# RWKV-6 attention followed by a squared-ReLU feed-forward: attention products in two groups per step, block-diagonal pair state, two shared PSUM banks, whole-group casts

## The chip, the cores and the metric

One core of one Trainium2 chip. The metric is the device time of one execution in microseconds (us); the time of a kernel is the median of its runs. Engines are called as in the profile: PE (TensorE; PEld its weight loads), DVE (VectorE), ACT (ScalarE), POOL (GpSimd), SP (SyncE, which here issues the DMAs).

## The reference, cut to what matters

```python
# r, k, v, w: (4 batches, 8 heads, 768 positions, 48); u: (8, 48)
for t in range(S):
    cur = einsum('bhd,bhe->bhde', u * k[t], v[t])
    y[t] = einsum('bhd,bhde->bhe', r[t], state + cur)
    state = w[t][..., None] * state + einsum('bhd,bhe->bhde', k[t], v[t])
x = y.transpose(0, 2, 1, 3).reshape(3072, 384)
out = relu(x @ w_in) ** 2 @ w_out        # w_in (384, 2048), w_out (2048, 384)
```

Inputs and output are float32; the products run in bfloat16 with float32 sums.

## The kernel before, in words

The 4 x 768 positions are cut into 12 steps of 256 (`T`), three per batch (`NB = 3`); a step is two chunks (`c`) of 64 partitions with two neighbouring positions (`j`) on each partition. The heads go in four pairs (`HP`, index `p`, head of the pair `e`), each head padded from 48 to 64 rows (`DP`).

**Attention of one step s.** `ww_`, `rw_`, `kw_` multiply decays into w, r and k; `lw_` takes the logarithm; `cum_` (L213) sums the logarithms on PE; `exp_` (L222) makes decay factors, and the chunk's total decay `a_c`; `rd_` (L229) writes the decayed r and k into `rdec`. `tr_`/`rkt_` transpose them through PSUM for steps 0 to 3, `dtr_` (L256) by a DMA transpose from step 4 on. `p_` (L261) forms k-times-r products for two head pairs at once in 64x64 tiles, `pm_` (L273) masks them. `su_` (L281) sums k-times-v over a chunk, one 64x64 product per head; `ts_` (L295) adds the old state, `sn_` (L303) multiplies by `a_c` on POOL and gives the next state `S`, two heads one above the other, 48 columns each. `y_` (L329) adds the inner products (mask times v, 32 products in 64x128 tiles) and, through `carried` (L320), the old state's share of the even heads (64x64 tiles); `yb_` adds the odd heads' share and the bonus term u (`ku_`, `qp_`, `q_`, `vq_`, then four `spread` products of 384 columns). For steps 0 and 1 a small DVE copy `yw_` stands between `y_` and `yb_`. `ysb_` evicts y; `yt_`/`xt_` (steps 0 to 3) or `dyt_` (L371, DMA transpose) turn it into x.

**Feed-forward (MoE) of one step.** `m1_` (L380): eight groups of 12 products with w_in; `rl_` relu, `sq_` square; `m2_` (L405): for each half of 128 rows four groups of four products with w_out; `os_` (L413) scales and evicts, `store` (L417) issues two DMAs on SP.

**PSUM.** `att` is two double banks; cum, p, su and y each take one and give it back after `rd_`, `pm_`, `ts_`, `ysb_`. One bank serves all transposes, two serve `m1_`, one serves `m2_` (and the warm-up products of L424, which fill PE's waits ahead of the first m2).

**Order.** All engines run in an order that is written when the kernel is built: `plan` (L431 to L550) lists every piece of work with engine, planned duration, rank, inputs and PSUM needs; `make_order` (L559) plays it through with these durations, on each engine taking the ready piece of lowest rank. Attention of step s has ranks around 200 s, its MoE 700 later. The order is then fixed: each engine works through its list, and a piece that waits holds up all behind it. Loads go through SP in the order `seq` (L525): steps 0 and 1 (w r u k v, w r k v), four w_in blocks, step 2, four w_out blocks, then steps 3 to 11. A load waits for the buffers of four steps earlier, and w of step n also for `y_(n - 3)`. On SP the ranks put transposes first, then stores, then loads. Weights come as float32 blocks of 768 KB and are cast a column group at a time: 12 casts for w_in, 16 for w_out, on ACT or DVE (L113).

Of the kernel before, what the change touches and what calls it, by code (L numbers as in the profile page):

```python
# [18 lines left out]
def kernel(  # L19
# [17 lines left out]
    C = 128  # L37
# [75 lines left out]
    def cast(kind, g, j):  # L113
        dst = wi_sb[:, :, g * GW:(g + 1) * GW] if kind == "i" else wo_sb[:, g * 4:(g + 1) * 4, :]
        copy = nc.scalar.copy if where["cast", kind, g, j] == "A" else nc.vector.tensor_copy
        copy(dst[:, j], w_st[kind, g][:, j])
# [34 lines left out]
    for i in range(NLW):  # L151
        t = consts.tile([C, H, DP], BF16, name=f"lw_buf{i}")
        nc.gpsimd.memset(t[:], 0.0)
        lw_bufs.append(t)
    NRD = 2
# [27 lines left out]
    def v_(s):  # L183
        v_bf = tiles["v", s] = a_mid.tile([C, H, 2, D], BF16, name="v_bf", bufs=3)
        nc.scalar.copy(v_bf[:], raw["v", s][:])  # L185
# [36 lines left out]
    def exp_(s):  # L222
        cs = tiles["cs", s]
        a_c = tiles["a_c", s] = a_small.tile([C, HP, 2], FP32, name="a_c")
        nc.scalar.activation(
            a_c[:], cs[:, 0, DM:DM + 2 * HP].rearrange("p (a c) -> p a c", c=2), AF.Exp)
        nc.scalar.activation(cs[:, :, 0:DM], cs[:, :, 0:DM], AF.Exp)  # L227

    def rd_(s, i):  # L229
        if i == 0:  # L230
            tiles["rdec", s] = rdec_bufs[s % NRD]
        rdec, cs = tiles["rdec", s], tiles["cs", s]
        x = raw["rk"[i], s][:, :, 0:3:2, :]
        nc.vector.tensor_mul(  # L234
            rdec[:, i, :, :, 0:D], x.rearrange("p h j d -> p j h d"),
            cs[:, i, 0:DM].rearrange("p (h d) -> p h d", h=H)[:, None, :, :].to_broadcast([C, 2, H, D]))
        if i == 1:
            del tiles["cs", s]

    def tr_(s, i):  # L240
        rdec = tiles["rdec", s]
        ps_tr = tiles["tr", s] = ps_tr_pool.tile([C, 2, HP, C], BF16, name="tr")
# [4 lines left out]
    def new_rkt(s, i):  # L247
        if i == 0:
# [3 lines left out]
    def rkt_(s, i):  # L252
        copy = nc.scalar.copy if where["rkt_", s, i] == "A" else nc.vector.tensor_copy
        copy(new_rkt(s, i)[:, i], tiles.pop(("tr", s))[:])
# [18 lines left out]
    def pm_(s, f):  # L273
        if f == 0:
# [5 lines left out]

    def su_(s):  # L281
        rdec, v_bf = tiles["rdec", s], tiles["v", s]
        ps_su = tiles["su", s] = att[slot["su_", s]]
        n_c = 1 if s % NB == NB - 1 else 2
        for j in range(2):
            for p in range(HP):
                for c in range(n_c):
                    for e in range(2):
                        part = slice(c * Q, (c + 1) * Q)
                        nc.tensor.matmul(ps_su[e * DP:(e + 1) * DP, c, p * D:(p + 1) * D],  # L290
                                         rdec[part, 1, j, 2 * p + e, :], v_bf[part, 2 * p + e, j, :],
                                         start=(j == 0 and p == 0), stop=(j == 1),
                                         skip_group_check=True)

    def ts_(s, c):  # L295
        ps_su = tiles["su", s][:, c, 0:HP * D].rearrange("p (a d) -> p a d", a=HP)
        ts = tiles["ts", s, c] = a_mid.tile([C, HP, D], FP32, name="t_state")
        if s % NB == 0 and c == 0:
            nc.vector.tensor_copy(ts[:], ps_su)
        else:  # L300
            nc.vector.tensor_add(ts[:], tiles["S", s, c][:], ps_su)  # L301

    def sn_(s, c):  # L303
        t = tiles["S", s + c, 1 - c] = a_mid.tile([C, HP, D], BF16, name="S", bufs=6)
        nc.gpsimd.tensor_mul(t[:], tiles.pop(("ts", s, c))[:],  # L305
                             tiles["a_c", s][:, :, c:c + 1].to_broadcast([C, HP, D]))


# [10 lines left out]

    def carried(s, e):  # L320
        rows = slice(e * DP, (e + 1) * DP)
        for p in range(HP):
            h = 2 * p + e
            for c in range(0 if s % NB else 1, 2):
                for j in range(2):
                    y_mm(s, c, slice(h * D, (h + 1) * D), tiles["rkT", s][rows, 0, j, p, c * Q:(c + 1) * Q],
                         tiles["S", s, c][rows, p, :], j)

    def y_(s):  # L329
# [10 lines left out]
        carried(s, 0)  # L340

    def yw_(s):
        seen = a_small.tile([1, 2], FP32, name="seen")
        nc.vector.tensor_copy(seen[:], tiles["y", s][0:1, :, 0])

    def yb_(s):
        vq = tiles.pop(("vq", s))
        carried(s, 1)
# [10 lines left out]
    def yt_(s):  # L359
        y_sb = tiles.pop(("ysb", s))  # L360
        ps_yt = tiles["yt", s] = ps_tr_pool.tile([C, 2, KT, C], BF16, name="tr")
# [4 lines left out]
    def xt_(s):  # L366
        xT = tiles["xT", s] = xt_pool.tile([C, 2, KT, C], BF16, name="xT")
        copy = nc.scalar.copy if where["xt_", s] == "A" else nc.vector.tensor_copy
        copy(xT[:], tiles.pop(("yt", s))[:])
# [35 lines left out]
    def m2_(s, c, q):  # L405
        gt = tiles["gt", s]
        if q == 0:
            tiles["m2"] = ps_m2.tile([C, DM], FP32, name="m2")
        for n in range(4 * q, 4 * q + 4):
            nc.tensor.matmul(tiles["m2"][:], gt[:, n, c * C:(c + 1) * C], wo_sb[:, n, :],  # L410
                             start=(n == 0), stop=(n == NT - 1))

    def os_(s, c):  # L413
        o_sb = tiles["o", s, c] = o_pool.tile([C, DM], FP32, name="o_sb")
        nc.scalar.activation(o_sb[:], tiles.pop("m2")[:], AF.Copy, scale=1.0 / (RS * RS))  # L415

    def store(s, c):  # L417
# [3 lines left out]
        for j in range(2):  # L421
            nc.sync.dma_start(out=rows[j], in_=o_sb[j * Q:(j + 1) * Q, :])

    def warm_(n):  # L424
        ps = ps_m2.tile([C, 512], FP32, name="m2")
        for _ in range(n):
            nc.tensor.matmul(ps[:], warm[:, 0:C], warm[:], start=True, stop=True)  # L427
# [3 lines left out]
    plan = {}  # L431
    slot = {}
    where = {}

    def op(eng, us, rank, fn, args, deps, take=(), give=None, dma=None):
        key = (fn.__name__,) + args
        plan[key] = (eng, us, rank, fn, args, deps, take, give, dma)
# [4 lines left out]
    def by_dma(s):  # L442
        return s >= DMA_FROM

    def tr_done(s):

        return [] if s < 0 else [("dtr_" if by_dma(s) else "tr_", s, 1)]

    for s in range(NS):
        i, at = s % NB, s * 200  # L450
        ge = dict(V=.55) if s == 0 else dict(G=1.0)
        op(ge, None, at - 95, ww_, (s,), [("ld", s, "w")] + on("lw_", s - 2))
        op("A", .52, at - 60, lw_, (s,), [("ww_", s)] + on("cum_", s - NLW))
# [24 lines left out]
        op("P", .75, at + 3, y_, (s,),
           [("pm_", s, 0), ("pm_", s, 1), ("v_", s), ("sn_", s, 0)]
           + (on("sn_", s - 1, 1) if i else []), take=("att",))  # L480
        if s < SEEN:
            op("V", .15, at - 86, yw_, (s,), [("y_", s)])
        op("P", .55, at + 1, yb_, (s,), [("yw_" if s < SEEN else "y_", s), ("vq_", s)])
        op(dict(V=.95, A=.85), None, at - 85, ysb_, (s,),
           [("yb_", s)] + (on("dyt_", s - 2) if by_dma(s - 2) else on("yt_", s - 2)), give="att")
        if by_dma(s):
            op("S", 1.0, -2, dyt_, (s,), [("ysb_", s)] + on("m1_", s - 4, 7), dma=(48, 1.2, 1.3))
        else:
            op("P", .4, at + 2, yt_, (s,), [("ysb_", s)], take=("tr",))
            op(dict(A=.83, V=.55), None, at - 95, xt_, (s,), [("yt_", s)] + on("m1_", s - 4, 7), give="tr")  # L490
# [203 lines left out]
```

## Time and profile before

| | |
|---|---|
| median of 3 runs | 200.79 us (200.4 to 201.8) |
| the profiled execution's own time | 200.29 us |
| its span | 198.5 us |
| granted PE clock | 1.00 |
| busy | PE 95%, DVE 67%, ACT 56%, POOL 55% |
| moved by DMA | 36.24 MB |

The profile is of one execution. The span lies inside the time: 1.8 us of the 200.29 are around it. Busy shares are means over the whole span and say little about stages; busy PE includes the warm-up products. In the lists of groups a row has line, engine, operation, output <- inputs, shapes and count, then busy us and mean ns of one, then idle time of the engine ahead of them and what ended it. In the timelines a row has start, duration, engine, line and count; neighbouring matmul rows overlap, because a matmul's duration runs to its modelled end.

### The profile page before, as it was taken

To read this page: it belongs to the slowest core of one execution; us is meant where nothing else is said; L and a number is where in the kernel's file an instruction comes from. 1 tells how busy PE (TensorE), PEld (TensorE's weight loads), DVE (VectorE), ACT (ScalarE), POOL (GpSimd) and SP (SyncE) were. 2 spreads that over 40 slices of the span, in tenths; PEclk is the share of its full clock that TensorE was granted. 3 is DMA by queue.
4 is the path that set the end of the run, shared out by engine and by line. 5 is a ranking of instruction groups with operands and counts; after the bars stand their busy time and mean duration, and the time that the engine had idled before them with its cause. 6 is when DMAs were issued, how large, how long until landed. Compare 5 with 4: busy or idle time off the path is not lost.

```text
span 198.5 us, 6153 instructions
## 1 busy us (share of the span) xinstructions
PE 188.4 (95%) x2631; PEld 128.0 (64%) x2637; DVE 133.4 (67%) x189; ACT 111.2 (56%) x179; POOL 108.5 (55%) x108
## 2 busy tenths in 40 slices
PE   7679999999999999999999999999999999999981
PEld 2335676666767676676767677676676767777750
DVE  5667889986787695937668594686876556555520
ACT  2434987987973477738785664683661433323300
POOL 7199769459998997874758958349610000000000
PEclk9999999999999999999999999999999999999999
DMA  6999999999998949979999999899853312111132
GB/s 158 257 261 358 353 235 340 360 254 247 254 259 193 257 113 206 212 161 222 200 222 241 149 229 185 200 214 185 176 78 76 79 43 54 29 39 40 40 73 48
DMA packets 80939, 36.24 MB, mean 183 GB/s; under 512 B 74128, under 2 KB 79376, under 8 KB 80912
## 3 DMA queue, kind: packets, MB, share of 16 engines
q1 hardware_dynamic: 80912, 35.86, 82.1%
q8 instruction: 20, 0.33, 0.7%
q14 instruction: 7, 0.06, 0.1%
HBM read 25.36 MB, written 4.72 MB: 152 GB/s over the span
## 4 chain that ended last, share of the span: by engine, by line
PE 65%; DMA 15%; SPq 7%; issue 5%; POOL 4%; ACT 2%; DVE 1%; POOLq 0%; ACTq 0%
PE m L410 27%; PE m L386 24%; PE att L315 6%; DMA w_raw<-in_w_dram 6%; DMA w_st<-in_moe_w_in_dram 5%; SPq L93 5%; PE att L270 2%; DMA v_raw<-in_v_dram 2%; DMA k_raw<-in_k_dram 2%; PE att L290 1%; SPq L103 1%; ACT o_sb L415 1%; POOL ku L202 1%; POOL ku L197 1%; PE att L219 1%
## 5 line engine op out<-in xcount | busy, mean ns | idle before, releaser
L386 PE MATMUL m<-xT,wi_sb 128*128 128x256 bf16 x576 | 76.7, 273 | 0.2 <-DVE rl L395 0.2
L410 PE MATMUL m<-wo_sb,gt 128*128 128x384 bf16 x384 | 75.8, 327 | 0.8 <-ACT o_sb L415 0.8
L386 PEld LDWEIGHTS <-wi_sb 128*128 128x128 bf16 x576 | 54.5, 98 | 15.3 <-issue 1.8
L395 DVE TENSOR_SCALAR rl<-m 128x512 f16<-128x512 f32 x49 | 33.6, 689 | 33.7 <-PE m L386 33.5
L410 PEld LDWEIGHTS <-gt 128*128 128x128 bf16 x384 | 35.3, 98 | 20.5 <-issue 2.5
L393 ACT ACTIVATE rl<-m 128x512 f16<-128x512 f32 x47 | 27.9, 596 | 34.9 <-PE m L386 34.5
L276 DVE TENSOR_TENSOR pmT<-att,mask 128x1024 bf16<-128x1024 f32 x24 | 28.4, 1216 | 2.2 <-ACT gt L401 1.0
L401 ACT ACTIVATE gt<-rl 128x1024 bf16<-128x1024 f16 x25 | 26.4, 1057 | 5.5 <-DVE rl L395 5.0
L197 POOL TENSOR_TENSOR ku<-k_raw,u_bc 128x768 f32<-128x768 f32 x12 | 22.6, 1882 | 4.7 <-DMA k_raw<-in_k_dram 4.7
L210 POOL TENSOR_TENSOR vq<-v_raw,q 128x768 bf16<-128x768 f32 x12 | 18.0, 1501 | 12.2 <-PE att L270 3.4
L202 POOL TENSOR_TENSOR ku<-ku,r_raw 128x768 f32<-128x768 f32 x12 | 21.8, 1814 | 0.6
L415 ACT ACTIVATE o_sb<-m 128x384 f32<-128x384 f32 x24 | 11.7, 488 | 17.1 <-PE m L410 16.7
L403 DVE TENSOR_TENSOR gt<-rl 128x1024 bf16<-128x1024 f16 x23 | 18.8, 819 | 2.3 <-ACT rl L393 0.6
L177 POOL TENSOR_TENSOR ww<-w_raw 128x384 f32<-128x384 f32 x11 | 11.0, 1002 | 12.8 <-DMA w_raw<-in_w_dram 12.8
L427 PE MATMUL m<-warm 128*128 128x512 bf16 x55 | 15.9, 414 | 1.3 <-DVE half_ones L145 1.2
L305 POOL TENSOR_TENSOR S<-t_state,a_c 128x192 bf16<-128x192 f32 x20 | 11.1, 556 | 7.3 <-DVE t_state L301 6.2
L185 ACT CAST v_bf<-v_raw 128x768 bf16<-128x768 f32 x12 | 10.0, 831 | 6.5 <-DMA v_raw<-in_v_dram 6.3
L234 DVE TENSOR_TENSOR rdec_buf<-r_raw,att 128x768 bf16<-128x768 f32 x12 | 11.4, 950 | 3.0 <-ACT att L227 2.0
L193 POOL TENSOR_TENSOR k_raw<-k_raw,w_raw 128x384 f32<-128x384 f32 x11 | 11.3, 1026 | 1.7 <-DMA k_raw<-in_k_dram 1.7
L206 DVE TENSOR_REDUCE q<-ku 128x16 f32<-128x768 f32 x12 | 11.3, 943 | 1.2 <-POOL ku L202 1.2
L189 POOL TENSOR_TENSOR r_raw<-r_raw,w_raw 128x384 f32<-128x384 f32 x11 | 11.6, 1051 | 0.5 <-DMA r_raw<-in_r_dram 0.5
L234 DVE TENSOR_TENSOR rdec_buf<-k_raw,att 128x768 bf16<-128x768 f32 x12 | 11.3, 946 | 0.0
(64 smaller groups left out, 163.5 us busy)
## 6 DMA issues: line engine op xcount, KB each, us to landing
w_raw<-in_w_dram SPq DMA_DIRECT2D x12, 384.0 KB, 5.8
r_raw<-in_r_dram SPq DMA_DIRECT2D x12, 384.0 KB, 6.3
k_raw<-in_k_dram SPq DMA_DIRECT2D x12, 384.0 KB, 6.4
v_raw<-in_v_dram SPq DMA_DIRECT2D x12, 384.0 KB, 6.0
out_dram<-o_sb SPq DMA_DIRECT2D x48, 96.0 KB, 2.3
w_st<-in_moe_w_in_dram SPq DMA_DIRECT2D x4, 768.0 KB, 8.9
w_st<-in_moe_w_out_dram SPq DMA_DIRECT2D x4, 768.0 KB, 8.6
rkT<-rdec_buf SPq DMA_TRANSPOSE x16, 4.5
```

The source lines that it names most:

```text
L197: nc.gpsimd.tensor_mul(ku[:], raw["k", s][:, :, 1:3, :], u_bc[:, :, None, :].to_broadcast([C, H, 2, D]))
L202: nc.gpsimd.tensor_mul(ku[:], ku[:], raw["r", s][:, :, 0:2, :])
L210: nc.gpsimd.tensor_mul(vq[:].rearrange("p j h d -> p h j d"), raw["v", s][:], tiles.pop(("q", s))[:, :, :, None].to_broadcast([C, H, 2, D]))
L234: nc.vector.tensor_mul(rdec[:, i, :, :, 0:D], x.rearrange("p h j d -> p j h d"), cs[:, i, 0:DM].rearrange("p (h d) -> p h d", h=H)[:, None ...
L276: nc.vector.tensor_mul(tiles["pmT", s][:, f].rearrange("p a j t -> p a (j t)"), tiles.pop(("p", s, f))[:].rearrange("p e (a x) -> p (e a) ...
L386: nc.tensor.matmul(ps1[:, j, :], wi_sb[:, kk, n * 128:(n + 1) * 128], tiles["xT", s][:, :, kk, :], start=(kk == 0), stop=(kk == KT - 1))
L393: nc.scalar.activation(rl, m1[:], AF.Relu, scale=RS)
L395: nc.vector.tensor_scalar(out=rl, in0=m1[:], scalar1=RS, scalar2=0.0, op0=ALU.mult, op1=ALU.max)
L401: nc.scalar.activation(gt, rl[:], AF.Square)
L403: nc.vector.tensor_mul(gt, rl[:], rl[:])
L410: nc.tensor.matmul(tiles["m2"][:], gt[:, n, c * C:(c + 1) * C], wo_sb[:, n, :], start=(n == 0), stop=(n == NT - 1))
L427: nc.tensor.matmul(ps[:], warm[:, 0:C], warm[:], start=True, stop=True)
```

## The change

- `su_` takes a head pair in one product (64 rows, 128 x 96 outputs): 16 products instead of 32 for two chunks. The off-diagonal head blocks hold sums that nobody wants; `a_c` is now a buffer (`ac_bufs`) zeroed once, into which `exp_` writes only the diagonal blocks by two activations, so `sn_` multiplies the others by zero. State sums and state have 384 columns instead of 192.
- The carried product uses all 128 rows of a pair at once (`yc_`: 128x64 tiles, 96 columns, 16 products instead of 32).
- From step 3 (`COMP`) on PE's work of a step comes as two groups, each one piece of the plan: `pp_` (both halves of p; takes both `att` banks) and `yy_` (su of the next step, inner products, spread products, carried product; takes both `att` banks).
- Transposes and m2 share two banks `bk` (before: one each). su of step 0 uses the two m1 banks. `yw_` is gone.
- A weight block is cast by one instruction, on ACT, DVE or POOL. `v_` may run on POOL, and `ww_`, `rw_`, `kw_` on DVE, for steps 0 to 2.
- The last output tile is scaled half by ACT, half by DVE, and its second store is issued on ACT's queue.
- The plan has new durations, a cost of 0.09 for changing PE's tile shape, `NUDGE` (a table of some 200 additions to ranks), a new load order, and MoE ranks 730 behind attention; `m2_` is ranked 250 (before: 200) behind `m1_`.

```diff
@@ su_, ts_, sn_
+        if s == 0:
+            ps_su = tiles["su", s] = [ps_m1.tile([C, 512], FP32, name="m1") for _ in range(2)]
+        else:
+            ps_su = tiles["su", s] = [att[slot["su_", s]][:, c, :] for c in range(2)]
         for j in range(2):
             for p in range(HP):
                 for c in range(n_c):
-                    for e in range(2):
-                        part = slice(c * Q, (c + 1) * Q)
-                        nc.tensor.matmul(ps_su[e * DP:(e + 1) * DP, c, p * D:(p + 1) * D],
-                                         rdec[part, 1, j, 2 * p + e, :], v_bf[part, 2 * p + e, j, :],
+                    part = slice(c * Q, (c + 1) * Q)
+                    nc.tensor.matmul(ps_su[c][:, p * 2 * D:(p + 1) * 2 * D],
+                                     rdec[part, 1, j, 2 * p:2 * p + 2, :], v_bf[part, 2 * p:2 * p + 2, j, :],
...
-        ts = tiles["ts", s, c] = a_mid.tile([C, HP, D], FP32, name="t_state")
+        ts = tiles["ts", s, c] = a_mid.tile([C, DM], FP32, name="t_state")
...
-        t = tiles["S", s + c, 1 - c] = a_mid.tile([C, HP, D], BF16, name="S", bufs=6)
+        t = tiles["S", s + c, 1 - c] = a_mid.tile([C, HP, 2, D], BF16, name="S", bufs=6)
@@ exp_
+        for e in range(2):
+            rows = slice(e * DP, (e + 1) * DP)
+            nc.scalar.activation(
+                a_c[rows, :, :, e], cs[rows, 0, DM:DM + 2 * HP].rearrange("p (a c) -> p a c", c=2), AF.Exp)
@@ carried product and groups
+    def pp_(s):
+        p_(s, 0)
+        p_(s, 1)
...
+    def yc_(s):
+        for c in range(0 if s % NB else 1, 2):
+            for p in range(HP):
+                for j in range(2):
+                    y_mm(s, c, slice(2 * p * D, (2 * p + 2) * D),
+                         tiles["rkT", s][:, 0, j, p, c * Q:(c + 1) * Q],
+                         tiles["S", s, c][:, p].rearrange("p e d -> p (e d)"), j)
+
+    def yy_(s):
+        if s + 1 < NS:
+            su_(s + 1)
+        y_(s)
+        yq_(s)
+        yc_(s)
@@ end
+        if (s, c) == (NS - 1, 1):
+            half = DM // 2
+            nc.scalar.activation(o_sb[:, 0:half], m2[:, 0:half], AF.Copy, scale=1.0 / (RS * RS))
+            nc.vector.tensor_scalar_mul(o_sb[:, half:DM], m2[:, half:DM], 1.0 / (RS * RS))
...
+            queue = nc.scalar if (s, c, j) == (NS - 1, 1, 1) else nc.sync
@@ order
+    NUDGE = {("cast", "i", 0): -300, ("cast", "i", 3): -50, ("cast", "o", 0): -110, ("cast", "o", 1): -5,
...
+        ("pm_", 0): -700, ("pm_", 2): -60, ("pm_", 3): -700, ("pm_", 5): -100, ("pm_", 6): 20,
...
+    SEQ = [(0, "w"), (1, "w"), (0, "r"), (0, "k"), (0, "v"), (0, "u"), (1, "k"), (1, "r"), (1, "o"),
+        (0, "i"), (1, "v"), (2, "i"), (1, "i"), (3, "i"), (0, "o"), (2, "w"), (2, "r"), (2, "k"), (2, "v"),
+        (2, "o"), (3, "w"), (3, "o"), (3, "r"), (3, "k"), (3, "v"), (5, "r"), (4, "w"), (4, "k"), (4, "r"),
...
+    SET = dict(lead=3, ahead=730, after=250, ri=120, ro=620, leave=0.0, same=20)
...
+            if s >= COMP:
+                op("P", .5, at + 5, pp_, (s,), [(rkt, s, 0), (rkt, s, 1)],
+                   take=(("att", ("p_", s, 0)), ("att", ("p_", s, 1))))
...
+            state = [("sn_", s, 0)] + (on("sn_", s - 1, 1) if i else [])
+            inner = [("pm_", s, 0), ("pm_", s, 1), ("v_", s)]
...
+                op("P", (1.53 if i else 1.36) - (0 if more else .34), at + 3, yy_, (s,),
+                   inner + state + [("vq_", s)] + ([("rd_", s + 1, 1), ("v_", s + 1)] if more else []),
+                   take=((("att", ("su_", s + 1)),) if more else ()) + (("att", ("y_", s)),))
```

More of the change, by code (lines that the diff above doesn't have):

```diff
@@ L154 @@
         lw_bufs.append(t)
+    NAC = 4
+    ac_bufs = []
+    for i in range(NAC):
+        t = consts.tile([C, HP, 2, 2], FP32, name=f"ac_buf{i}")
+        nc.gpsimd.memset(t[:], 0.0)
+        ac_bufs.append(t)
     NRD = 2
@@ L247, in new_rkt @@
     def new_rkt(s, i):
-        if i == 0:
+        if ("rkT", s) not in tiles:
             tiles["rkT", s] = a_mid.tile([C, 2, 2, HP, C], BF16, name="rkT")
@@ L273, in pm_ @@
     def pm_(s, f):
-        if f == 0:
+        if ("pmT", s) not in tiles:
             tiles["pmT", s] = a_mid.tile([C, 2, 4, 2, C], BF16, name="pmT")
@@ L318 @@
     begun = set()
[L320 to L327, printed above, removed]
     def y_(s):
@@ L421, in store, with warm_ @@
         for j in range(2):
-            nc.sync.dma_start(out=rows[j], in_=o_sb[j * Q:(j + 1) * Q, :])
-    def warm_(n):
-        ps = ps_m2.tile([C, 512], FP32, name="m2")
+            queue = nc.scalar if (s, c, j) == (NS - 1, 1, 1) else nc.sync
+            queue.dma_start(out=rows[j], in_=o_sb[j * Q:(j + 1) * Q, :])
+    def warm_(n, i):
         for _ in range(n):
[L427 to L433, printed above, removed]
+            nc.tensor.matmul(bk[i][:], warm[:, 0:C], warm[:], start=True, stop=True)
@@ L563, in make_order @@
[L563 removed]
+        psum = {x: [(0.0, i) for i in range(n)]
+                for x, n in dict(att=2, bk=2, m1=2, rl=3).items()}
+        waits, users, needs = {}, {}, {}
         for key in plan:
[L565 to L570 removed]
+            waits[key] = list(dict.fromkeys(plan[key][5]))
+            needs[key] = collections.Counter(x[0] if type(x) is tuple else x for x in plan[key][6])
+            for d in waits[key]:
+                assert d in plan, (key, d)
+                users.setdefault(d, []).append(key)
@@ new lines, in make_order, with offer @@
+        left = {key: len(waits[key]) for key in plan}
+        todo, begin = {e: [] for e in free_at}, {}
+        number = {key: i for i, key in enumerate(plan)}
+        def offer(key):
+            for e in plan[key][0]:
+                begin[key, e] = max(
+                    [0.0] + [issued[d] if plan[key][3] is ld and d[0] == "ld"
+                             else done[d] + (HOP if where[d] != e else 0) for d in waits[key]])
+                bisect.insort(todo[e], (plan[key][2], number[key], key))
@@ L578, in make_order @@
         done, order, times = {}, [], [0.0, .74, 1.5, 3.5]
-        dma_free, queue = 0.0, []
-        while any(todo.values()):
+        dma_free, queue, mode = 0.0, [], "m"
+        for key in plan:
+            if not left[key]:
+                offer(key)
+        while len(order) < len(plan):
             now = heapq.heappop(times)
@@ L584, in make_order @@
                     continue
-                for key in todo[e]:
-                    _, us, _, fn, _, _, take, give, dma = plan[key]
-                    def ready(d):
-                        if fn is ld and d[0] == "ld":
-                            return d in issued
-                        return d in done and done[d] + (HOP if where[d] != e else 0) <= now + 1e-6
-                    if not all(ready(d) for d in waits[key]):
-                        continue
-                    if us is None and e in "AV" and len(plan[key][0]) == 2:
-                        other = "V" if e == "A" else "A"
-                        if (max(now + HOP, free_at[other]) + cost(key, other, now) + LEAVE
-                                < now + cost(key, e, now)):
-                            continue
-                    if not all(psum[x] and min(psum[x])[0] < now + 1e-6 for x in take):
+                items = todo[e]
@@ L601, in make_order @@
                         continue
-                    if fn is yb_ and key[1] >= SEEN and engine_seen["P"] < count["y_", key[1]]:
+                    if not all(len(psum[x]) >= n and sorted(psum[x])[n - 1][0] < now + 1e-6
+                               for x, n in needs[key].items()):
                         continue
-                    known = [seen[d] for d in waits[key]
-                             if not (fn is ld and d[0] == "ld") and not (e == where[d] == "P")]
+                    end = now + cost(key, e, now)
```

373 lines of the change are left out of this document (208 added, 165 removed), and 7 rows, old and new, of tables (NUDGE, SEQ).

## The prediction, made before the change was run

> **What bounds the kernel now.** I read the page's busy shares first, then busy time by stage, then the list of groups, then TensorE's timeline, and last the DMA queue. In the table by stage a row has the stretch, its length, then busy time (and instructions) of PE, of its weight loads, of DVE, ACT and POOL, and the granted clock; the second stretch begins with the first MoE product.
>
> ```profile
> span 198.5 us, 6153 instructions
> PE 188.4 (95%) x2631; PEld 128.0 (64%) x2637; DVE 133.4 (67%) x189; ACT 111.2 (56%) x179; POOL 108.5 (55%) x108
> ```
> ```profile
> 0.00:23.56 23.56, 19.20 (x243) 9.69 (x248) 15.65 (x33) 11.08 (x18) 16.54 (x30) 1.00 1.01 277
> 23.56:50.00 26.44, 25.72 (x388) 18.32 (x390) 22.39 (x34) 21.75 (x38) 19.07 (x15) 1.00 1.05 288
> 50.00:150.00 100.00, 99.81 (x1586) 69.39 (x1584) 73.28 (x94) 64.33 (x101) 72.95 (x65) 1.00 1.02 197
> ```
> From 50 to 150 us TensorE (PE) is idle for 0.19 us, at a granted clock of 1.00: that stretch is pure TensorE time. The other engines have a quarter of it or more to spare. Before 50 us PE looks busy too, but the warm-up products (line 427) are in it:
>
> ```profile
> 0.00:23.56 23.56, 13.30 (x45) 4.64 (x49) 1.00 1.01 277
> 23.56:50.00 26.44, 2.65 (x10) 1.13 (x12) 1.00 1.05 288
> ```
> So real work is 188.4 - 13.30 - 2.65 = 172.5 us. The other 26.0 of the span are 21.0 at the start (15.95 of warm-up, 4.36 + 0.72 idle), 0.2 in the middle, and what is left, 4.8, at the end. The time changes with these two sums, and with nothing else as long as PE stays the bound.
>
> **The attention products.** One stretch of PE's timeline holds all the groups of a step (start, duration; I use differences of starts, because neighbours overlap):
>
> ```profile
> 82.20 0.42 PE L270 MATMUL att<-rkT 64*64 64x128 bf16 x16
> 82.55 1.47 PE L410 MATMUL m<-wo_sb,gt 128*128 128x384 bf16 x8
> 83.95 0.44 PE L290 MATMUL att<-v_bf,rdec_buf 64*64 64x48 bf16 x32
> 84.32 0.82 PE L410 MATMUL m<-wo_sb,gt 128*128 128x384 bf16 x4
> 85.08 0.57 PE L315 MATMUL att<-v_bf,pmT 64*128 64x48 bf16 x32
> 85.58 0.43 PE L315 MATMUL att<-S,rkT 64*64 64x48 bf16 x16
> 85.95 1.48 PE L410 MATMUL m<-wo_sb,gt 128*128 128x384 bf16 x8
> 87.26 1.47 PE L386 MATMUL m<-xT,wi_sb 128*128 128x256 bf16 x12
> 88.57 0.24 PE L217 MATMUL att<-half_ones,lw_buf 128*128 128x2 bf16 x4
> 88.67 0.32 PE L219 MATMUL att<-lw_buf,tri_strict 128*128 128x384 bf16 x1
> 88.83 0.32 PE L220 MATMUL att<-lw_buf,tri_incl_neg 128*128 128x384 bf16 x1
> 89.00 0.82 PE L386 MATMUL m<-xT,wi_sb 128*128 128x256 bf16 x6
> 89.74 0.43 PE L315 MATMUL att<-S,rkT 64*64 64x48 bf16 x16
> 90.11 0.50 PE L315 MATMUL att<-vq,spread 64*128 64x384 bf16 x4
> 90.54 0.83 PE L386 MATMUL m<-xT,wi_sb 128*128 128x256 bf16 x6
> ...
> 97.10 0.31 PE L315 MATMUL att<-S,rkT 64*64 64x48 bf16 x8
> 97.33 0.83 PE L386 MATMUL m<-xT,wi_sb 128*128 128x256 bf16 x6
> ...
> 104.00 0.64 PE L270 MATMUL att<-rkT 64*64 64x128 bf16 x32
> 104.58 0.66 PE L410 MATMUL m<-wo_sb,gt 128*128 128x384 bf16 x3
> ```
> Eight L410 products take 1.31 us ahead of another full-array group (85.95 to 87.26) and 1.40 ahead of a small-tile group (82.55 to 83.95): entering costs 0.1. The carried product falls from 0.37 (16) to 0.23 (8): 0.034 a pair and 0.10 fixed, so leaving a tile shape costs 0.1 too. One step now costs, with entries: two p groups 2 x 0.45 (82.20 to 82.55, plus 0.1), su 0.47, y 0.97, yb 0.90, together 3.24.
>
> After, from step 3 on, there are two groups. **pp**: the row at 104.00 is it, 0.58 + 0.10 against 0.90, so 0.22 less. This trace already has p undivided in three of those nine steps, hence 6 x 0.22 = 1.3. **yy**: no row shows its su and carried forms (64x128 and 128x64 tiles, 96 columns). L219 takes 0.16 for 384 columns, so 0.04 for 96; 16 products as 8 simultaneous pairs are 0.32. The inner products are 0.50 less 0.10, the spread 0.43 less 0.10. yy = 0.32 su + 0.40 + 0.33 + 0.32 carried + 0.3 (entry, one change of shape, leaving) = 1.67, against 0.47 + 0.97 + 0.90 = 2.34: 0.67 less. By steps: 5 and 8, 2 x 0.67; 3, 6, 9 (half the carried product: 2.07 to 1.51), 3 x 0.56; 4, 7, 10 (the next su has half the products, which now cost half: 2.33 to 1.51), 3 x 0.82; 11 (no su: 1.87 to 1.35), 0.52. That is 6.0; steps 0 to 2, not grouped, 0.2. **Term: -7.5.** Bounds: if pairs do not run side by side, su and carried cost 0.64 each; with 6.5 su and 7.5 carried equivalents, 14 x 0.32 = 4.5 come back (-3.0). At 0.034 a pair it is 14 x 0.05 more (-8.2). I take pairs, since every two-tile row above shows them.
>
> **What grows and is hidden.** State sums double to 384 columns and a state product doubles too:
>
> ```profile
> L301 DVE TENSOR_TENSOR t_state<-S,att 128x192 f32<-128x192 bf16 x16 | 5.6, 348 | 3.5 <-POOL S L305 2.4 <-PE att L290 1.1
> L305 POOL TENSOR_TENSOR S<-t_state,a_c 128x192 bf16<-128x192 f32 x20 | 11.1, 556 | 7.3 <-DVE t_state L301 6.2 <-ACT gt L401 0.9 <-DVE t_state L299 0.2
> L177 POOL TENSOR_TENSOR ww<-w_raw 128x384 f32<-128x384 f32 x11 | 11.0, 1002 | 12.8 <-DMA w_raw<-in_w_dram 12.8
> L234 DVE TENSOR_TENSOR rdec_buf<-r_raw,att 128x768 bf16<-128x768 f32 x12 | 11.4, 950 | 3.0 <-ACT att L227 2.0 <-PE att L315 0.8
> ```
> Between 348 ns (192) and 950 (768) a state sum comes to 0.55: +0.2 x 20 = 4 us of DVE. On POOL 0.56 becomes 1.0 as in L177: +9 us, 73% to about 79% of the middle stretch. I cost both at nothing: PE's 13 us per step cover them. Uncovered, two sums and two products add 1.3 us per step to the state chain, 14 us in all. The added exponential (8 elements) and the 28 casts that become 8 lie under the same cover.
>
> **The end.**
>
> ```profile
> 191.49 2.76 PE L410 MATMUL m<-wo_sb,gt 128*128 128x384 bf16 x16 [0.58 <-ACT o_sb L415]
> 194.29 0.49 ACT L415 ACTIVATE o_sb<-m 128x384 f32<-128x384 f32 x1 [2.85 <-PE m L410]
> 194.81 1.11 SPq L422 DMA_DIRECT2D out_dram<-o_sb  x2
> ```
> A second bank removes the 0.58 (and most of the middle's 0.19). Half a scaling on each of ACT and DVE saves about 0.15 of 0.49 (estimated, fixed cost kept). The second store's issue, half of 1.11, moves to ACT's queue, where nothing follows: 0.55. **Term: -1.5**, bounds -1.6 to -0.6 (the queue gives nothing).
>
> **The start.**
>
> ```profile
> 13.08 0.95 DVE L206 TENSOR_REDUCE q<-ku 128x16 f32<-128x768 f32 x1 [1.21 <-POOL ku L202]
> 13.95 2.34 DVE L276 TENSOR_TENSOR pmT<-att,mask 128x1024 bf16<-128x1024 f32 x2
> ```
> DVE waited 1.21 us for the bonus sum q and ran it 0.9 us ahead of step 0's masks; the change ranks step 0's masks 700 earlier, ahead of q, so the first x, and the first MoE product at 23.56, could come 2.1 earlier. Against it stands SP's queue. w of step 1 (384 KB) goes ahead of r and k of step 0, and u (192 KB) behind v: 192 KB more ahead of k, 0.7 us at 277 GB/s. A 768 KB block of w_out stands ahead of the first w_in block where v of step 1 was: 384 KB, 1.4 us later weights. Step 2's loads stand behind six weight blocks instead of four, so fewer attention inputs are ready at 30 us. **Term: -1.5**, bounds -4 (2.1 and over half of the 3.4 unreal us after 23.56) and +2 (1.4 and a late cast).
>
> **New waits.** yy(s) waits for masks, vq(s), both states, and for rd and v of step s+1, and takes both attention banks; pp takes both too. Behind it on PE's in-order queue stand all MoE products, and relu, squares and stores wait for those. In the old order PE waited 0.19 us in the middle. **Term: +0.8**, four times that, as each of the two groups waits for the inputs of two or three old ones and for both banks. Bounds: 0 (as now), and +5.3 if every fourth of the 18 groups comes a whole mask late (1.17, half of the 2.34 at 13.95).
>
> **Sum** against the profiled execution's own 200.29: -7.5 - 1.5 - 1.5 + 0.8 = -9.7, 190.6. The median, 200.79, lies 0.50 higher; the same difference gives **191.1 us**.
>
> **Rivals.**
>
> Everything lands well: -8.2 - 1.6 - 4 + 0 gives 187.0. For it: the nearly waitless middle. Against: w_in does not land sooner.
>
> The wider products do not pair: 191.1 + 4.5 = 195.6. For it: no row has these shapes. Against: p and the inner products pair.
>
> Weights are not hidden under the carried product, whose tiles now all span the same rows. A load's row is 0.098:
>
> ```profile
> L386 PEld LDWEIGHTS <-wi_sb 128*128 128x128 bf16 x576 | 54.5, 98 | 15.3 <-issue 1.8 <-DMA xT<-y_sb 0.4
> ```
> With 10 equivalents of 16 products, 160 x 0.098 = 15.7, giving 206.8. Against it: twelve L386 products with whole-array weights take 1.31 us (87.26), 0.109 each for 256 columns, so there the loads are hidden. The Trainium skill, TensorE: Matmul & The Clock Gate, section "Part 3: Packing small matmuls", says that a weight load overlaps running products only in another row group, which would bring about this rival; the L386 row contradicts it for the full array, and no row here shows it for column tiles.
>
> Slower, from the bank pair: pp and yy need both banks, so the attention becomes a ring: yy 1.6, eviction of y 0.9 (planned), cum 0.4 (88.57 to 89.00), exponentials 1.1 (planned), two rd 1.9, pp 0.6, two masks 2.3: 9 us without queueing. PE needs 13.3 per step: 4 x 1.31 for 48 L386 products, as much for 32 of L410, 0.4 and 2.35. So the ring sets the pace only when its seven handovers average over 0.6 us, and loses time on before from 0.75 on, a pace of 14.2.
>
> ```profile
> 49.77 0.69 SPq L93 DMA_DIRECT2D w_raw<-in_w_dram  x1
> 125.69 0.63 SPq L93 DMA_DIRECT2D w_raw<-in_w_dram  x1
> ```
> The attention pace is now 12.65 us per step (w loads of steps 5 to 11). A paced kernel ends at about 44 + 11 x pace (first x near 21.5, the rest the last step's 10.5 of products, their latency and the end): no gain at 14.2, 205 at 14.6. For it: masks and rd share DVE with relu. Against: DVE has 27% free.
>
> It does not do what it says: the order comes from planned times, and freed PE time falls where no MoE product is due, warm-up or idle growing by as much: about 200.5.
>
> **How the numbers follow.** Forecast 0.55; all well 0.17; no pairs 0.11; bank ring 0.06; weights not hidden 0.03; no effect 0.08. A measurement of this kernel tells about 1% from no change. Faster by over 1%: 0.83, within 1%: 0.08, slower: 0.09. The forecast alone spans 188 to 194 (sizes of start and waits); taking in both neighbouring cases the range is 186 to 198, leaving out the last three cases and a little of the second.
>
> **What would show it.** Right: PE's real work near 165; the 64x128 su rows and 128x64 carried rows at 0.04 a pair; pp near 0.58; PE idle under 1.5 us between 50 us and the end; first MoE product near 22; no 0.58 in the last step. Wrong: idle PE ahead of pp or yy behind a mask, rd or state; warm-up plus idle before 50 us above 23; DVE or POOL near 90% in the middle; a first MoE product after 25 us.

## The result and the profile after

The changed kernel takes **193.0 us** (median of 4 runs, 192.95 to 194.07; two more took 193.16 and 193.85), the kernel before, beside it on the same chip, 201.1 (200.4 to 201.8). The ratio is 0.961, 95% interval 0.957 to 0.965: 8.1 us less, where 9.7 was forecast; 191.1 was named, the range was 186 to 198. A few executions that took over 1.5% longer than the fastest of their kernel, most of them at a lower granted clock, are left out of medians and ratios, except in the fourth experiment, where they are the finding.

The profiled execution of the changed kernel took 194.07 us, 1.1 more than the median, with a span of 192.3. The same kernel was profiled once more later (the fifth run below) with a span of 191.2, so two profiles stand for "after". Some lines of the first profile's page, then busy time by stage (columns as in the prediction):

```profile
PE 181.6 (94%) x2313; PEld 127.1 (66%) x2317; DVE 138.5 (72%) x175; ACT 118.7 (62%) x189; POOL 112.7 (59%) x107
...
L317 POOL TENSOR_TENSOR S<-t_state,ac_buf 128x384 bf16<-128x384 f32 x20 | 18.8, 939 | 19.3 <-DVE t_state L312 16.5
...
L443 PE MATMUL bk<-warm 128*128 128x512 bf16 x57 | 16.1, 417 | 1.6 <-DVE half_ones L145 1.2
```
```profile
0.00:50.00 50.00, 44.07 (x516) 28.47 (x521) 43.13 (x62) 33.58 (x47) 32.71 (x43) 1.00 1.03 284
50.00:160.00 110.00, 109.25 (x1552) 78.60 (x1550) 81.39 (x95) 76.41 (x126) 80.02 (x65) 1.00 0.96 185
160.00:192.30 32.30, 28.26 (x251) 20.07 (x249) 13.97 (x20) 8.75 (x17) 0.00 (x0) 1.00 0.21 50
```
The same view of the second profile of this kernel:

```profile
0.00:50.00 50.00, 44.33 (x517) 28.62 (x522) 43.34 (x62) 33.15 (x47) 32.81 (x43) 1.00 1.04 287
50.00:160.00 110.00, 109.78 (x1559) 79.29 (x1557) 79.84 (x95) 77.30 (x128) 80.10 (x65) 1.00 0.95 184
160.00:191.20 31.20, 27.20 (x243) 19.23 (x240) 13.08 (x19) 7.91 (x15) 0.00 (x0) 0.97 0.22 51
```
Warm-up products are taken out of PE's busy time as before the change: 181.6 - 16.1 = 165.5 of real work, in the second profile 181.3 - 16.3 = 165.0. Each stretch's length less its busy time is the idle time.

| part of the span, us | before | after | after, second profile | forecast of the difference |
|---|---|---|---|---|
| PE, real work | 172.5 | 165.5 | 165.0 | -7.5 |
| before 50 us: idle and warm-up | 21.0 | 22.0 | 22.0 | -1.5 |
| idle in the middle | 0.2 | 0.75 | 0.2 | +0.8 |
| idle at the end | 4.8 | 4.0 | 4.0 | -1.5 |
| span | 198.5 | 192.3 | 191.2 | -9.7 |

So nearly the whole gain is PE work; the start did not get shorter but 1.0 longer, and half of the end's term came. PE's timeline over one step of the changed kernel, with the shorter carried product of a later step behind the gap (start, duration, as in the prediction):

```profile
84.13 1.47 PE L397 MATMUL m<-xT,wi_sb 128*128 128x256 bf16 x12
85.53 0.51 PE L302 MATMUL att<-v_bf,rdec_buf 64*128 64x96 bf16 x16
85.88 0.56 PE L325 MATMUL att<-v_bf,pmT 64*128 64x48 bf16 x32
86.28 0.48 PE L325 MATMUL att<-vq,spread 64*128 64x384 bf16 x4
86.70 0.53 PE L325 MATMUL att<-S,rkT 128*64 128x96 bf16 x16
87.16 1.48 PE L397 MATMUL m<-xT,wi_sb 128*128 128x256 bf16 x12
...
93.57 0.64 PE L275 MATMUL att<-rkT 64*64 64x128 bf16 x32
94.15 1.15 PE L420 MATMUL bk<-wo_sb,gt 128*128 128x384 bf16 x6
...
99.34 0.36 PE L325 MATMUL att<-S,rkT 128*64 128x96 bf16 x8
99.63 1.48 PE L397 MATMUL m<-xT,wi_sb 128*128 128x256 bf16 x12
```
The group yy is the four rows from 85.53 to 87.16, 1.63, and 0.09 of entry: the twelve L397 products ahead take 1.40 to the start of su instead of their 1.31. That is 1.72, against 1.67 forecast. The group pp is 93.57 to 94.15, 0.58 as forecast. The carried product takes 0.46 with 16 products and 0.29 with 8, so 0.0425 a pair and 0.12 fixed; su takes 0.35 for its eight pairs.

At the start, PE, then DVE, then POOL, all of the changed kernel:

```profile
17.96 0.57 PE L325 MATMUL att<-v_bf,pmT 64*128 64x48 bf16 x32 [1.27 <-DVE pmT L281]
...
21.67 0.50 PE L325 MATMUL att<-vq,spread 64*128 64x384 bf16 x4
...
25.25 1.47 PE L397 MATMUL m<-xT,wi_sb 128*128 128x256 bf16 x12
```
```profile
9.14 0.55 DVE L199 TENSOR_TENSOR k_raw<-k_raw,w_raw 128x384 f32<-128x384 f32 x1
...
13.04 1.22 DVE L281 TENSOR_TENSOR pmT<-att,mask 128x1024 bf16<-128x1024 f32 x1
14.17 2.13 DVE L199 TENSOR_TENSOR k_raw<-k_raw,w_raw 128x384 f32<-128x384 f32 x1
...
16.69 1.21 DVE L281 TENSOR_TENSOR pmT<-att,mask 128x1024 bf16<-128x1024 f32 x1
17.83 0.94 DVE L212 TENSOR_REDUCE q<-ku 128x16 f32<-128x768 f32 x1
```
```profile
11.31 1.82 POOL L203 TENSOR_TENSOR ku<-k_raw,u_bc 128x768 f32<-128x768 f32 x1 [6.82 <-DMA u_bc<-in_u_dram]
...
14.09 1.81 POOL L208 TENSOR_TENSOR ku<-ku,r_raw 128x768 f32<-128x768 f32 x1
...
17.64 1.82 POOL L203 TENSOR_TENSOR ku<-k_raw,u_bc 128x768 f32<-128x768 f32 x1
19.41 1.80 POOL L216 TENSOR_TENSOR vq<-v_raw,q 128x768 bf16<-128x768 f32 x1
```
Step 0's first mask does run 0.9 earlier (13.04 instead of 13.95). But step 1's k product, now DVE's, stands between the two masks and takes 2.13 us beside POOL's product of 14.09, where the same product alone took 0.55 at 9.14. The second mask starts at 16.69 and the inner products at 17.96. The bonus sum q, now behind both masks, starts at 17.83 (before the change 13.08). Then the spread product waits for vq, and vq on POOL stands behind q and behind step 1's ku (17.64); POOL itself had waited 6.82 for u, which is loaded later now. The first MoE product starts at 25.25, where "near 22" was called right and "after 25" wrong.

The end:

```profile
188.29 0.33 ACT L428 ACTIVATE o_sb<-bk 128x192 f32<-128x192 f32 x1 [2.11 <-PE bk L420]
188.66 0.36 DVE L429 TENSOR_SCALAR o_sb<-bk 128x192 f32<-128x192 f32 x1 [7.32 <-ACT o_sb L428]
189.05 0.55 ACTq L439 DMA_DIRECT2D out_dram<-o_sb  x1
```
PE's 0.58 wait in the last step is gone. The two halves of the scaling run one behind the other: DVE's was released by ACT's, and together they take 0.7 instead of 0.49.

### The profile page after: what moved, and what is told of

The parts are those of the page before. It is cut to its first block, busy times and chain, and to the rows that moved or that the text cites. A ratio compares the mean times of both kernels' runs of the same rounds, so it can differ in the third digit from the quotient of the medians.

```text
span 192.3 us, 5508 instructions
## 1 busy us (share of the span) xinstructions
PE 181.6 (94%) x2313; PEld 127.1 (66%) x2317; DVE 138.5 (72%) x175; ACT 118.7 (62%) x189; POOL 112.7 (59%) x107
## 5 line engine op out<-in xcount | busy, mean ns | idle before, releaser
L397 PE MATMUL m<-xT,wi_sb 128*128 128x256 bf16 x576 | 71.7, 273 | 0.0
L420 PE MATMUL bk<-wo_sb,gt 128*128 128x384 bf16 x384 | 70.7, 326 | 0.2 <-ACT gt L412 0.2
L397 PEld LDWEIGHTS <-wi_sb 128*128 128x128 bf16 x576 | 55.0, 98 | 11.6 <-DMA xT<-y_sb 0.2
L404 ACT ACTIVATE rl<-m 128x512 f16<-128x512 f32 x64 | 37.5, 595 | 26.5 <-PE m L397 25.4
L406 DVE TENSOR_SCALAR rl<-m 128x512 f16<-128x512 f32 x32 | 21.8, 689 | 16.0 <-PE m L397 16.0
L317 POOL TENSOR_TENSOR S<-t_state,ac_buf 128x384 bf16<-128x384 f32 x20 | 18.8, 939 | 19.3 <-DVE t_state L312 16.5
L414 DVE TENSOR_TENSOR gt<-rl 128x1024 bf16<-128x1024 f16 x24 | 23.9, 997 | 4.9 <-ACT rl L404 3.9
L208 POOL TENSOR_TENSOR ku<-ku,r_raw 128x768 f32<-128x768 f32 x12 | 22.7, 1893 | 0.5
L431 ACT ACTIVATE o_sb<-bk 128x384 f32<-128x384 f32 x23 | 11.1, 485 | 10.7 <-PE bk L420 10.5
L443 PE MATMUL bk<-warm 128*128 128x512 bf16 x57 | 16.1, 417 | 1.6 <-DVE half_ones L145 1.2
L367 DVE CAST y_sb<-att 128x768 bf16<-128x768 f32 x9 | 8.6, 956 | 8.0 <-PE att L325 8.0
L183 POOL TENSOR_TENSOR ww<-w_raw 128x384 f32<-128x384 f32 x9 | 9.1, 1006 | 8.2 <-DMA w_raw<-in_w_dram 8.2
```

The lines of the kernel that those rows point to most:

```text
L208: nc.gpsimd.tensor_mul(ku[:], ku[:], raw["r", s][:, :, 0:2, :])
L317: nc.gpsimd.tensor_mul(t[:], tiles.pop(("ts", s, c))[:].rearrange("p (a e d) -> p a e d", a=HP, e=2), tiles["a_c", s][:, :, c, :, None].to ...
L397: nc.tensor.matmul(ps1[:, j, :], wi_sb[:, kk, n * 128:(n + 1) * 128], tiles["xT", s][:, :, kk, :], start=(kk == 0), stop=(kk == KT - 1))
L404: nc.scalar.activation(rl, m1[:], AF.Relu, scale=RS)
L406: nc.vector.tensor_scalar(out=rl, in0=m1[:], scalar1=RS, scalar2=0.0, op0=ALU.mult, op1=ALU.max)
L414: nc.vector.tensor_mul(gt, rl[:], rl[:])
```

## The experiments

Theory: PE's work sets the time, and the gain is the cheaper shapes. Rivals: the order, the load order or the new tail earned it; and for what was missing, the late first x against the landing of the weights.

**One: three needless changes of shape put into yy** (a two-column full-array product behind su, inner and spread products, into columns that nobody reads).

```diff
+        def touch():
+            nc.tensor.matmul(att[slot["y_", s]][:, 0, 400:402], warm[:, 0:C], warm[:, 0:2],
+                             start=False, stop=True, skip_group_check=True)
```


> Changed kernel with its order kept; in each group yy three small full-array products (2 columns, into columns of the y bank that nothing reads) force PE to leave and enter a tile shape again: behind su, behind the inner products, behind the spread products. Theory (PE's own work sets the time, entering and leaving a shape cost 0.1 us each): 8 x 0.23 + 9 x 0.23 + 9 x 0.13 = 5.1 us more of PE work and of time, about 198. Rival (the groups leave PE with slack, the attention ring or the loads set the time): less than 1 us more.

197.5 us (median of nine, two of them 200.2), ratio to before 0.990 (0.987 to 0.994): 4.5 over the changed kernel's 193.0. Its step:

```profile
86.20 0.51 PE L302 MATMUL att<-v_bf,rdec_buf 64*128 64x96 bf16 x16
86.65 0.18 PE L359 MATMUL att<-warm 128*128 128x2 bf16 x1
...
88.37 1.48 PE L404 MATMUL m<-xT,wi_sb 128*128 128x256 bf16 x12
```
The group takes 2.17 instead of 1.63, 0.18 for each touch; PE's real work grows by 4.0 to 4.5 (186.0 - 16.5 = 169.5 against 165.5 and 165.0), the time by 4.5. PE sets the time, and grouping without leaving the small shapes is worth what the shape changes cost.

**Two: the groups undone** (new shapes, new start and tail, `COMP = 3` set to 12, planned anew).

> Changed kernel, but no step has the groups pp and yy: p, su, y, spread and carried products are planned one by one in all 12 steps, as in steps 0 to 2; the order is planned anew. Theory (grouping is most of the PE saving): PE's real work rises from 165.4 by 3 to 7 us, depending on how many pieces end up apart, and the time rises by as much, 196 to 200. Rival (the wider products carry the saving): PE's real work stays within 1.5 us of 165.4 and the time within 2 us of 193.

196.9, ratio 0.986 (0.981 to 0.990): 3.9 over the changed kernel.

```profile
PE 184.8 (95%) x2313; PEld 126.6 (65%) x2317; DVE 141.4 (73%) x182; ACT 116.5 (60%) x182; POOL 111.8 (57%) x107
```
Less 16.4 of warm-up that is 168.4, so 3 more than with groups. Theory held, at its low end: grouping is 3 of the 7 us.

**Three: the wide shapes alone, in the kernel before with its old order** (su by head pairs, whole rows in the carried product, states of 384 columns).

```diff
-                    for e in range(2):
-                        part = slice(c * Q, (c + 1) * Q)
-                        nc.tensor.matmul(ps_su[e * DP:(e + 1) * DP, c, p * D:(p + 1) * D],
...
+                    part = slice(c * Q, (c + 1) * Q)
+                    nc.tensor.matmul(ps_su[:, c, p * 2 * D:(p + 1) * 2 * D],
```


> Kernel before with its own order, with only the block-diagonal state: su by head pairs, the carried product by whole rows and all of it in y_, state sums and products of 384 columns. Theory (widening alone saves little): per step su +0.08, carried +0.09 in y, carried part out of yb -0.37, so -0.2 x 12 = -2.4 us of PE work, about 198.5. Rival (widening carries most of the saving): -5 us or more, below 196. Second rival (the longer state sums on DVE and POOL, 13 us in all, are not covered): no gain or slower, 200 to 203.

200.15, ratio 0.999 (0.996 to 1.001): no change.

```profile
0.00:50.00 50.00, 44.52 (x546) 27.29 (x551) 38.92 (x65) 32.10 (x58) 36.51 (x48) 1.00 1.02 281
50.00:160.00 110.00, 109.84 (x1529) 75.93 (x1528) 83.33 (x103) 70.86 (x116) 79.11 (x65) 1.00 0.96 185
```
```profile
L307 DVE TENSOR_TENSOR t_state<-S,att 128x384 f32<-128x384 bf16 x16 | 8.8, 550 | 4.2 <-POOL S L311 3.1
...
L431 PE MATMUL m<-warm 128*128 128x512 bf16 x57 | 17.2, 430 | 1.2 <-DVE half_ones L145 1.2
```
PE's real work does fall, to 187.15 - 17.2 = 170.0, 2.5 less. The doubled state sums (0.55 each) and products hide: PE is idle for 0.16 us in the middle. But 5.5 idle and 17.2 of warm-up before 50 us make 22.7, 1.7 more than before, so most of the saving came back as start. PE's real work in these 50 us is 1.65 less (44.52 - 17.19 against 44.93 - 15.95), yet no more of the MoE is done in them: 90 products with w_in and 28 with w_out, before the change 90 and 30. This is the "no effect" rival in small: PE work saved early on is worth nothing if no MoE product is due. Of the 7.0 to 7.5 us of PE work that the whole change saves, grouping is about 3 (run two) and the wide shapes in the old order 2.5; the rest was not separated.

**Four: the start put right by hand** (step 1's k product to POOL, vq of step 0 ahead of step 1's ku, step 0's eviction and transposes ahead of step 1's second half, step 1's su behind the first two MoE groups, two warm-up runs of 13 and 8 products shortened to 6 and 5).

```diff
+    where["kw_", 1] = "G"
...
+            (("kw_", 1), ("vq_", 0)), (("ku_", 1), ("kw_", 1)),
...
+    for x, n in ((("yc_", 0), 6), (("p_", 0, 1), 5)):
```


> Changed kernel with its order kept from the second MoE group on; only step 0's bonus chain is freed: the k product of step 1 goes from DVE to POOL, step 0's vq ahead of step 1's ku on POOL, eviction and transposes of step 0 ahead of step 1's second rd, su of step 1 behind the first MoE groups, and ten fewer warm-up products. Theory (the late first x, 25.25 us for the first MoE product, is time lost at the end): first MoE product near 22.3, time 190 to 192. Rival (the landing of the w_in blocks and step 1's attention hold the next MoE groups anyway): first MoE product earlier, the time within 0.5 us of 193.

Its profiled execution took 192.9 us at a clock of 1.00, its five timed runs 195.8 to 195.9 at 0.991. PE:

```profile
21.15 0.49 PE L375 MATMUL bk<-ident,y_sb 128*128 128x128 bf16 x6 [1.10 <-ACT rkT L259]
...
23.23 1.03 PE L397 MATMUL m<-xT,wi_sb 128*128 128x256 bf16 x8 [1.13 <-ACT xT L380]
```
The first MoE product comes 2.0 earlier and buys nothing; two idle gaps of 1.1 us stand where warm-up products were. 0.009 of 194 us is 1.7 of the 3 us lost in the timed runs; the rest is open.

**Five and six: the changed kernel again, and the fourth with its gaps filled** (5 and 5 warm-up products at the two gaps, 8 instead of 6 after the carried product).

```diff
+    keys.insert(keys.index(("tr_", 1, 0)) + 1, ("warm_", 5, 1 - slot["tr_", 1, 0]))
+    keys.insert(keys.index(("tr_", 1, 1)) + 1, ("warm_", 5, 2))
```


> The changed kernel once more, beside the next three on one chip. Theory (its runs are as even as those of before): every run at a granted clock near 1.00 and 192 to 194 us. Rival (it too drops to 0.991 in some runs, as the kernel with the freed bonus chain did): some runs near 195.

192.9, ratio 0.964 (0.961 to 0.967). Of its six executions one, 196.5, came at a clock of 0.991 and one at 0.66, though the two gaps are not in this kernel.

> The kernel with the freed bonus chain, and in its PE gaps of the start (behind the carried product, behind step 1's first and second transposes) 2, 5 and 5 more warm-up products. Theory (its runs at 195.8 us and a mean clock of 0.991 came from PE standing idle between 18 and 23 us, after which PE ran slowly for a while): all runs at a clock near 1.00 and 191 to 193 us. Rival 1 (the clock falls for another reason): runs near 195.8 again. Rival 2 (the late first x costs nothing at the end): clock 1.00, but the time within 0.5 us of the changed kernel's.

192.7 (192.6 to 193.8), ratio 0.963 (0.961 to 0.966), the granted clock 0.995 to 1.00. So the lower clock is likelier with the gaps: five of six executions have it with them, none of six with the gaps filled, two of twelve in the changed kernel. The gaps don't force it, for the profiled execution of the fourth run has them at 1.00; the other five have no trace. And the early first product (22.95, 2.3 earlier) moves the end by nothing that can be told. What holds instead, on ACT and then on PE:

```profile
26.51 0.59 ACT L404 ACTIVATE rl<-m 128x512 f16<-128x512 f32 x1
```
```profile
22.95 1.47 PE L397 MATMUL m<-xT,wi_sb 128*128 128x256 bf16 x12
...
26.65 0.42 PE L275 MATMUL att<-rkT 64*64 64x128 bf16 x16 [0.68 <-DVE pmT L281]
27.00 0.82 PE L443 MATMUL bk<-warm 128*128 128x512 bf16 x3
27.66 0.82 PE L397 MATMUL m<-xT,wi_sb 128*128 128x256 bf16 x6
...
48.42 0.61 PE L250 MATMUL bk<-ident,rdec_buf 128*128 128x128 bf16 x8 [1.21 <-DVE rkT L259]
```
The first two MoE groups are early; the third, at 27.66, is only 0.55 ahead of the changed kernel's (28.21). Ahead of it on PE's fixed list stand step 1's second p, which waited for DVE's mask, and three warm-up products, which end after the first relu (27.10) has. That relu, behind a cast whose w_in block came at 25.13, looks like a second holder; run nine decides. At 48.42 nothing of the lead is left: both kernels' PE starts the same transposes of step 3 there. DVE's square ahead of them ends at 46.90 in both, though it begins 0.45 earlier here, beside a POOL product that ends at 46.35 in both; and POOL has worked almost without pause since w of step 3 came, for which it waited 2.1 us in the changed kernel (to 39.89) and 2.6 here (to 40.05). So that load probably ends the lead; this was not tested.

**Seven: the last tile split by rows, DVE's half in a tile of its own** (on top of the sixth).

```diff
+            nc.scalar.activation(o_sb[0:Q, :], m2[0:Q, 0:DM], AF.Copy, scale=1.0 / (RS * RS))
+            nc.vector.tensor_scalar_mul(o_two[Q:C, :], m2[Q:C, 0:DM], 1.0 / (RS * RS))
```


> As the kernel before this one, and the last output tile split by rows, each half into a tile of its own. Theory (DVE's half waited for ACT's because both write one tile): both halves start together, the last scaling ends about 0.2 us earlier, the time falls by 0.2 us. Rival (they wait because they read one PSUM bank): DVE's half still starts behind ACT's and, as each half is longer by rows, the end comes 0.3 us later.

192.85, ratio 0.963 (0.961 to 0.966). The halves still run in a row, as the rival had it; its later end does not show in the time:

```profile
186.93 0.48 ACT L428 ACTIVATE o_sb<-bk 64x384 f32<-64x384 f32 x1 [2.11 <-PE bk L420]
...
187.44 0.56 DVE L429 TENSOR_SCALAR w_st<-bk 64x384 f32<-64x384 f32 x1 [7.48 <-ACT o_sb L428]
```
Neither output nor rows are shared any more; what they still share is the PSUM bank that both read.

**Eight: the table of additions emptied** (`NUDGE = {}`).

> Changed kernel with no rank additions at all; products, groups, costs and load order as changed. Theory (the PE work carries the gain, the order carries little): PE's real work stays at 165.4, warm-up and idle grow by up to 3 us, 193 to 196. Rival (without the ranks the groups wait for their many inputs and the bank pair): PE idle of several us between 50 and 160 us, 198 or more.

197.3, ratio 0.985 (0.981 to 0.988), 4 over the changed kernel and between the two expectations.

```profile
0.00:50.00 50.00, 43.77 (x469) 27.28 (x474) 42.04 (x57) 32.89 (x49) 31.69 (x43) 1.00 1.05 285
50.00:160.00 110.00, 107.61 (x1544) 77.54 (x1544) 80.02 (x98) 73.51 (x123) 79.01 (x64) 1.00 0.92 183
```
The middle has 2.4 of idle time, 1.6 to 2.2 more than with the ranks; the start is 1.1 longer (6.2 idle, 16.9 of warm-up), PE's real work is 183.25 - 16.9 = 166.4, about 1 more. The ranks are worth 4 us, about half of it waits in the middle. Only one of these stands at a group: a yy that waits 0.74 for rd; the others are at a transpose, an x and a square (0.4 to 0.7 each).

**Nine: the w_in blocks ahead of the w_out blocks** (the sixth, with two w_out loads behind w_in and the first of step 2's loads, and the casts in the new order).

```diff
+    put(("ld", 1, "o"), ("ld", 2, "r"))
+    put(("ld", 0, "o"), ("ld", 2, "k"))
```


> The kernel with the freed bonus chain and filled gaps, and the first weight loads in another order: the w_out block that stood ahead of the w_in blocks goes behind them and behind w and r of step 2, the second w_out block behind k of step 2; the first w_in block is cast where that w_out block was. Theory (after the first x, the landing of the w_in blocks holds the start: casts waited 0.55 and 1.5 us for them): no cast of w_in waits, warm-up and idle before 50 us fall by 1 to 2 us, the time is 191 to 192. Rival (then step 1's masks, or the later w_out blocks, hold PE instead): warm-up and idle stay within 0.7 us, the time within 0.5 us of the changed kernel's.

198.0, ratio 0.987 (0.980 to 0.993): 5 us slower. Four of the six executions came at a clock of 0.983 to 0.991; the two at 0.998 took 196.5 and 197.2, and the span of the profiled one, 195.4, is 3.4 over the sixth's. So 3.4 of the 5 are seen in the trace. ACT, PE, then PE's waits:

```profile
24.78 0.60 ACT L404 ACTIVATE rl<-m 128x512 f16<-128x512 f32 x1
...
30.10 1.47 ACT L116 CAST wo_sb<-w_st 128x1536 bf16<-128x1536 f32 x1 [3.37 <-DMA w_st<-in_moe_w_out_dram]
31.48 0.59 ACT L404 ACTIVATE rl<-m 128x512 f16<-128x512 f32 x1
33.72 1.47 ACT L116 CAST wo_sb<-w_st 128x1536 bf16<-128x1536 f32 x1 [1.65 <-DMA w_st<-in_moe_w_out_dram]
```
```profile
28.01 0.82 PE L397 MATMUL m<-xT,wi_sb 128*128 128x256 bf16 x6
```
```profile
PE m L397 <- ACT rl L404: 3.1, 2, 2.5
```
The first relu is 1.7 earlier now, yet the third MoE group starts 4.71 behind the first (23.30 to 28.01), exactly as in run six (22.95 to 27.66). So the relu and the cast ahead of it did not hold that group; step 1's mask and the fixed list did, again with a wait of 0.68 for the mask. The w_in casts between the first x and the third group no longer wait, those of w_out do, 5.0 us together, with relu behind them on ACT and PE behind relu. The rival's mechanism was right on both counts (masks, later w_out blocks), its number, within 0.5 us, was not.

**Ten: the tail undone** (the changed kernel, last tile scaled whole, both stores on SP's queue).

> Changed kernel, the last output tile scaled whole by ACT and both its stores issued on SP, as before. Theory (the split scaling costs 0.2 us, since its halves run one behind the other, and the second queue saves half a microsecond of issue): last scaling ends 0.2 us earlier, last store is issued 0.35 us later, time +0.3. Rival (the last landing follows the first store, not the second): no later end, time -0.2.

192.9 (192.75 to 193.06), ratio 0.961 (0.957 to 0.966): no difference in the time. In the trace PE's idle time at the end is 4.25 (191.3 - 160 - 27.05) against 4.0, so the split and the second queue are worth about 0.2 together.

## Why the prediction was right, and where it was not

**The attention products: right.** -7.5 was forecast, -7.0 and -7.5 are in the two profiles. Pairs in the unseen shapes run side by side at 0.0425, entering costs 0.09, a change of shape 0.1, pp is 0.58, yy 1.72 for 1.67. The rival without pairs falls with these rows. So does the one with weights not hidden: a load for them has 0.109 in the changed kernel's profile, 16 of them 1.7, and the 16 carried products took 0.46 in all. That this work sets the time is shown by runs one and two, which add 4 and 3 us of it and take 4.5 and 3.9 longer. The Trainium skill, TensorE: Matmul & The Clock Gate, section "Part 3: Packing small matmuls", has the rule weighed in the prediction, that a weight load overlaps running products only in another row group (the section also lets a load into a background weight buffer go ahead); the 0.46 contradicts that "only" for tiles that differ in columns alone, too.

**What grows and is hidden: right.** A state sum takes 0.55, a product 0.94, POOL is busy 79% of the time from 50 to 150 us, as forecast, and DVE 73 to 75%, and run three has the whole growth with 0.16 us idle there.

**The start: wrong, in the step "masks ahead of q, so the first MoE product 2.1 earlier".** The masks moved, but the gain was counted along one chain, with what the change sets in their way left out: step 1's k product on DVE (given no cost, 2.13 us), q behind both masks, u later, and vq behind step 1's ku. +1.0 instead of -1.5. Run four undoes the first and the last of these and has its first product 2.0 earlier. And the step was wrong twice: that earlier product is worth nothing with the rest of the order kept (run six), because the third MoE group stands behind step 1's masks and the fixed list, and what lead is left ends at step 3's transposes. The prediction's counterweight was later weights. Run nine shows that the w_in blocks did not hold the third group, and that w_out blocks hold relu when they are moved back. What would keep the lead stays open: an earlier w of step 3, a start with fewer weight bytes, and an order planned anew around the early x were not tried.

**The end: mis-sized.** -1.5 was made of the bank's 0.58 and 0.19, 0.15 for the split and 0.55 for the queue. -0.8 came: the bank's 0.58, gone from the last step, and about 0.2. Run ten shows the split and the queue at 0.2 together instead of 0.7, and run seven that the halves don't overlap by rows either; the 0.19 lay in the middle, where idle time did not fall.

**New waits: right in kind.** 0.0 to 0.6 more idle in the middle against +0.8. The bank ring never set the pace. Its low price rests on the ranks: without them it is 1.6 to 2.2 more (run eight).

**The sum.** From -9.7: 2.5 at the start, 0.7 at the end, up to 0.5 of PE work, less 0.2 to 0.8 for the waits, is the -6.2 and -7.3 of the two profiles. The medians' -8.1 holds 0.8 more than the second because the profiled execution of before, 200.29, was 0.8 below the median of the kernel in this comparison. So 0.8 of the 8.1, and of the closeness to 9.7, is luck: beside the repeat of run five the medians differ by 7.3 (200.15 and 192.9), as the second profile does. The forecast held because its large term was right; start and end together came to +0.2 instead of -3.0.

## What to carry to other kernels

Cost small-tile products by pairs that run at once plus 0.1 us for each change of tile shape, and grouping by the changes it saves; where PE is the bound, such a sum held within half a microsecond of seven. A gain at the start has to be followed past the first product to the second and third group of the main work, with everything that stands ahead of them in an in-order queue (a mask, planned filling, a cast that waits for its load), before it counts. A wait that looks like the holder is shown to be it only when it is taken away: here the relu came 1.7 earlier and nothing moved. A split of one tile over two engines has to be checked for overlap; here the halves ran one after the other.

## What the hardware showed beside that

- An f32 product of 128x384 on DVE took 0.55 us alone and 2.13 beside a POOL product: moving work to an idle engine cost four times its price. It looks held rather than slowed: in three rows of the changed kernel such a product ended 0.40 to 0.42 after the POOL product that ran when it began (16.30 after 15.90, 19.88 after 19.46, 36.10 after 35.68), whatever its own length (2.13, 1.19, 1.47).
- ACT and DVE reading one PSUM bank ran one after the other, by columns (0.33, then 0.36) and by rows with outputs of their own (0.48, then 0.56). Whether the bank or the order between the two instructions forces it was not separated.
- With two PE gaps of 1.1 us near 20 us, five of six executions came at a granted clock of 0.991 and 3 us longer; with warm-up products in the gaps none of six did (0.995 to 1.00).
